# Attention into a gated FFN on one core: the first batch in another order of loads, bias copies, masks and P V

## The chip, the cores and the metric

The kernel runs on one core of a Trainium2 chip. The metric is the time of one execution on the device, in microseconds (us). Three runs of the kernel before gave 438.77, 437.65 and 438.74, so a median of 438.74 us.

## What is computed

There are 8 batches of 8 heads, 576 positions and 64 numbers per head. Each head is a causal attention with a bias that falls with the distance between two positions, and its result, 4608 tokens by 512, goes through a gated FFN of width 1536:

```python
scores = q @ k.T / 8
cum = np.cumsum(np.maximum(s, 0), axis=-1)
scores += np.minimum(-(cum[:, None] - cum[None, :]), 0)   # and -1e9 above the diagonal
attn = softmax(scores) @ v
x = attn of all heads side by side                          # 4608 x 512
g = x @ w_gate
out = (g * sigmoid(g) * (x @ w_val)) @ w_out
```

## The kernel before

**The scores.** TensorE multiplies k (as weights) by q in one pass with a contraction of 128 rows: 64 rows hold k and q of a head, and 4 of the other 64 hold the bias. There the cumulative sum, times 8, stands as a coarse and a fine bf16 row (tile `HL`), against rows of 1 and -1, so that the product adds their difference. The tiles `KQ[i][e]` hold this: `i` is the buffer, `e` tells which half of the rows is q and k; one tile serves heads 0 and 2 of a group of four ("half batch", `hb`), the other heads 1 and 3. `aug` (L159) copies the bias rows of one half batch by DMA.

**One head** is four score pieces (L250), an exponential of each on ScalarE (L258), two masks of the diagonal blocks on GpSimd (L262, L267), then 15 small multiplications of the probabilities `pt` by V (L283, "P V"), whose last column of ones gives the row sums, and on VectorE a reciprocal and a multiplication (L298, L299). The PSUM tile of P V has one buffer, so that a head's P V waits until VectorE has read the one before. Every two heads, `x_pe` (L315) transposes the result into the FFN's input.

**Preparing k, q and V.** SyncE's queue (SP) loads them in fp32. GpSimd casts k and q to bf16 (`cast_one`, L174), TensorE transposes them (`pe_transpose`, L206), and VectorE and ScalarE copy them from PSUM to `KQ` (L217, L215). V is cast to the tile `VT` (L221). The buffer of raw V is single, those of raw k and q are double.

**The order** is written out by hand: each engine and each DMA queue takes its instructions in the order of the code. First come loads, memsets, the bias and half batch 0. Then `attn_items` gives the attention in pieces, and `pump` runs it up to a position. All eight heads of batch 0 run before the FFN's first tile of 512 tokens, since that tile needs all heads of its tokens; after that one piece of FFN (36 of them per tile) alternates with attention of the following batch. `side` holds what is issued beside a head: k and q of the next half batch, loads of V and the weights. The weights come in 12 DMAs from GpSimd's queue, which converts them from fp32 to bf16: four parts each of gate ("g"), value ("v") and output ("o").

Of the kernel before, what the change touches and what calls it, by code (L numbers as in the profile page):

```python
# [12 lines left out]
FP32 = mybir.dt.float32  # L13
# [6 lines left out]
def kernel(  # L20
# [79 lines left out]
    HL = const.tile([BH, 2, S], BF16)  # L100
    warm = const.tile([128, 1], FP32)

    with tc.manual_schedule():
# [30 lines left out]
        load_qk(0)  # L134
        load_v(0, range(5))
        load_qk(1)
# [184 lines left out]

        def side(h, step):
            if h == 0:
                if step == 0:
                    w_load("g", 1)
                    cast_one(1, "k", 0, nc.gpsimd)
                    cast_one(1, "q", 0, nc.gpsimd)
                if step == 1:
                    w_load("v", 1)
                    cast_one(1, "k", 1, nc.gpsimd)  # L330
                    cast_one(1, "q", 1, nc.gpsimd)
                if step in (2, 3):
                    for nm in ("k", "q"):
                        pe_transpose(1, nm, step - 2, (nc.vector, nc.vector))
                if step == 3:
                    w_load("g", 2)
                return
            if h == 1:
                if step == 0:
                    aug(2, nc.sync)  # L340
                    load_qk(2)
                    load_v(1, range(5))
                    w_load("v", 2)
                if step == 1:
                    w_load("g", 3)
                if step == 2:
                    w_load("v", 3)
                if step == 3:
                    w_load("o", 0)
# [36 lines left out]
        def attn_items():  # L386
            for kk in range(BH + 4):
                first = kk < H + 2
                bh = kk if first else kk - 2
                b_lo, b_hi = (0, H) if first else (H, BH)  # L390
                h, step = divmod(bh, HB)
                if not first and step == 0 and 2 <= h < NPE:
                    if h > 2:
                        aug(h, nc.sync)
# [19 lines left out]
                x = bh - 2  # L414
# [3 lines left out]
                p = bh - 1  # L418
# [137 lines left out]
```

## Time and profile before

| | |
|---|---|
| median of 3 runs | 438.74 us |
| the profiled execution | 440.81 us, of which the span from the first to the last instruction 439.1 us |
| TensorE busy | 394.4 us (90%) |
| VectorE, ScalarE, GpSimd busy | 265.7, 208.0, 138.8 us (61%, 47%, 32%) |
| chain that ended last | TensorE 84%, VectorE 10% |
| mean granted TensorE clock | 0.979 |

Engines are named PE (TensorE), DVE (VectorE), ACT (ScalarE), POOL (GpSimd) and SP (SyncE's queue). The page cuts the span into 40 slices of 11 us; a digit is the busy share of an engine in tenths. TensorE has `0538888696` in the first ten slices and 9 nearly everywhere after. VectorE has `7588` in the first four. The DMA engines stand at `8975999767` there. So the time in which TensorE isn't full lies in the first quarter, and the rows below come from there.

### The profile page before, as it was taken

To read this page: it belongs to the slowest core of one execution; us is meant where nothing else is said; L and a number is where in the kernel's file an instruction comes from. 1 tells how busy PE (TensorE), PEld (TensorE's weight loads), DVE (VectorE), ACT (ScalarE), POOL (GpSimd) and SP (SyncE) were. 2 spreads that over 40 slices of the span, in tenths; PEclk is the share of its full clock that TensorE was granted. 3 is DMA by queue.
4 is the path that set the end of the run, shared out by engine and by line. 5 is a ranking of instruction groups with operands and counts; after the bars stand their busy time and mean duration, and the time that the engine had idled before them with its cause. 6 is when DMAs were issued, how large, how long until landed. Compare 5 with 4: busy or idle time off the path is not lost.

```text
span 439.1 us, 8204 instructions
## 1 busy us (share of the span) xinstructions
PE 394.4 (90%) x3112; PEld 217.2 (49%) x3112; DVE 265.7 (61%) x507; ACT 208.0 (47%) x418; POOL 138.8 (32%) x249
## 2 busy tenths in 40 slices
PE   0538888696899999999999999999999999999996
PEld 0326545354455555555555555555555554444442
DVE  7588475634269637963794479448935762780760
ACT  1424447544455555555655555456555551332331
POOL 0753813446334423443262416241721110000000
PEclk9999899979699999999999999999999999999999
DMA  8975999767588659756965796577431001002002
GB/s 185 191 106 98 203 202 221 125 147 187 137 190 184 133 136 228 159 119 190 194 152 120 201 192 155 131 188 162 69 90 50 1 1 72 24 2 86 11 0 96
DMA packets 92679, 56.42 MB, mean 128 GB/s; under 512 B 65568, under 2 KB 87968, under 8 KB 92640
## 3 DMA queue, kind: packets, MB, share of 16 engines
q1 hardware_dynamic: 86672, 51.16, 51.5%
q0 software_dynamic: 5952, 4.73, 7.2%
q8 instruction: 24, 0.39, 0.4%
q14 instruction: 15, 0.12, 0.1%
q10 hardware_dynamic: 16, 0.01, 0.0%
HBM read 37.90 MB, written 15.93 MB: 123 GB/s over the span
## 4 chain that ended last, share of the span: by engine, by line
PE 84%; DVE 10%; ACT 2%; issue 2%; POOL 1%; DMA 0%; SPq 0%; ACTq 0%
PE py L459 22%; PE pv L448 21%; PE pg L435 21%; PE sc L250 9%; PE av L283 7%; DVE kq L217 4%; PE xps L315 3%; DVE vt L221 1%; DVE kq L148 1%; DVE kq L147 1%; ACT pt L258 1%; DVE ot L299 1%; DVE kq L146 1%; POOL kq L164 1%; DVE pp L442 0%
## 5 line engine op out<-in xcount | busy, mean ns | idle before, releaser
L258 ACT ACTIVATE pt<-sc 128x512 bf16<-128x512 f32 (+1 forms) x256 | 117.3, 504 | 68.2 <-PE sc L250 67.4
L448 PE MATMUL pv<-xt,wv 128*128 128x512 bf16 x432 | 113.3, 385 | 0.0
L435 PE MATMUL pg<-xt,wg 128*128 128x512 bf16 x432 | 112.6, 384 | 0.0
L442 DVE SCALAR_TENSOR_TENSOR pp<-th,pg 128x512 bf16<-128x512 bf16 x108 | 74.2, 687 | 61.1 <-ACT th L440 60.7
L440 ACT ACTIVATE th<-pg 128x512 bf16<-128x512 f32 x108 | 64.5, 597 | 90.7 <-PE pg L435 90.7
L459 PE MATMUL py<-wo,ht 128*128 128x512 bf16 x432 | 107.4, 384 | 0.0
L250 PE MATMUL sc<-kq 128*128 128x128 bf16 (+4 forms) x576 | 78.5, 253 | 11.7 <-DMA kq<-HL 4.7
L262 POOL TENSOR_SCALAR_AFFINE_SELECT pt<-pt 128x512 bf16<-128x512 bf16 x64 | 41.1, 642 | 141.3 <-ACT pt L258 141.2
L453 DVE TENSOR_TENSOR ht<-pp,pv 128x512 bf16<-128x512 bf16 x108 | 73.9, 684 | 13.0 <-PE pv L448 4.4
L250 PEld LDWEIGHTS <-kq 128*128 128x128 bf16 x576 | 48.0, 103 | 45.6 <-issue 6.5
L283 PE MATMUL av<-vt,pt 128*128 128x65 bf16 x960 | 51.8, 199 | 10.7 <-DVE ot L299 9.1
L448 PEld LDWEIGHTS <-wv 128*128 128x128 bf16 x432 | 39.3, 99 | 38.4 <-issue 4.1
L283 PEld LDWEIGHTS <-pt 128*128 128x128 bf16 x960 | 43.2, 101 | 29.2 <-issue 11.5
L435 PEld LDWEIGHTS <-wg 128*128 128x128 bf16 x432 | 38.8, 99 | 36.8 <-issue 1.8
L459 PEld LDWEIGHTS <-ht 128*128 128x128 bf16 x432 | 38.4, 99 | 35.8 <-issue 1.1
L467 ACT ACTIVATE ysb<-py 128x512 f32<-128x512 f32 x36 | 21.5, 597 | 44.8 <-PE py L459 42.7
L298 DVE RECIPROCAL rc<-av 128x5 f32<-128x5 f32 x64 | 12.2, 191 | 37.6 <-PE av L283 37.4
L267 POOL TENSOR_SCALAR_AFFINE_SELECT pt<-pt 128x64 bf16<-128x64 bf16 x64 | 15.3, 240 | 60.2 <-ACT pt L258 60.1
L299 DVE TENSOR_TENSOR ot<-av,rc 128x320 bf16<-128x320 f32 x64 | 31.5, 492 | 2.2
L319 DVE COPY xt<-xps 128x64 bf16<-128x64 bf16 (+7 forms) x32 | 9.8, 305 | 35.3 <-PE xps L315 35.3
L221 POOL CAST vt<-rawv 128x512 bf16<-128x512 f32 (+1 forms) x35 | 23.1, 677 | 10.9 <-DMA rawv<-in_v_dram 10.8
L174 POOL CAST ck<-rawk 96x768 bf16<-96x768 f32 x32 | 26.1, 833 | 0.0
(37 smaller groups left out, 174.9 us busy)
## 6 DMA issues: line engine op xcount, KB each, us to landing
rawk<-in_k_dram SPq DMA_DIRECT2D x16, 576.0 KB
rawq<-in_q_dram SPq DMA_DIRECT2D x16, 576.0 KB
out_dram<-ysb SPq DMA_DIRECT2D x36, 256.0 KB
rawv<-in_v_dram SPq DMA_DIRECT2D x32, 256.0 KB
ks<-ck SPq DMA_DIRECT2D x11, 288.0 KB
qs<-cq SPq DMA_DIRECT2D x11, 288.0 KB
kq<-HL SPq DMA_DIRECT2D x120, 2.2 KB
wg<-in_moe_w_gate_dram POOLq DMA_DIRECT2D x4, 384.0 KB, 5.3
```

The source lines that it names most:

```text
L221: eng.tensor_copy(VT[b % 2][0:n, c, :, 0:D], loaded["v", b][0:n, c, :, :])
L250: nc.tensor.matmul(sc[:, o : o + w], T[:, 0, r * S + 128 * tj : r * S + 128 * (tj + 1)], T[:, 1, r * S + lo : r * S + hi], start=True, sto ...
L258: nc.scalar.activation(pt[:, CHUNK_PT[ci] : CHUNK_PT[ci] + o], sc[:, 0:o], AF.Exp, scale=0.125)
L262: nc.gpsimd.affine_select(pt[:, 1088:1600], pt[:, 1088:1600], pattern=[[0, 4], [1, 128]], compare_op=ALU.is_ge, fill=zreg, base=0, channel ...
L283: nc.tensor.matmul(av[:, bi * (D + 1) : (bi + 1) * (D + 1)], pt[:, c0 : c0 + 128], VT[b % 2][:, tj, h, :], start=(tj == 0), stop=(tj == bi),)
L299: nc.vector.tensor_mul(ot[:, :, e * D : (e + 1) * D], av3[:, :, 0:D], rc[:, :, None].to_broadcast([128, NCH, D]),)
L435: nc.tensor.matmul(pg, WG[j][:, c, f0 : f0 + 128], xt[:, c, :], start=(c == 0), stop=(c == 3),)
L440: nc.scalar.activation(th, pg, AF.Tanh, scale=0.5)
L442: nc.vector.scalar_tensor_tensor(pp, in0=th, scalar=1.0, in1=pg, op0=ALU.add, op1=ALU.mult)
L448: nc.tensor.matmul(pv, WV[j][:, c, f0 : f0 + 128], xt[:, c, :], start=(c == 0), stop=(c == 3),)
L453: nc.vector.tensor_mul(ht, pp, pv)
L459: nc.tensor.matmul(py, hts[ft][:, ts_ * 128 : (ts_ + 1) * 128], WO[ft // 3][:, ft % 3, :], start=(ft == 0), stop=(ft == NFT - 1),)
```

## The change

It concerns the first batch and what is issued around it.

- `HL` gets four row pairs, so that one DMA per head carries the rows of the sum and those of 1 and -1, for k and q together (8 rows of 576 numbers); before it took two DMAs of 2 rows, and the 1 and -1 came from memsets.
- The memsets of `KQ` are cut down (fp32 writes of a pair of bf16 ones in one), partly moved to GpSimd, and partly placed later. VectorE's bias chain comes ahead of them.
- On SP k and q of half batch 1 load ahead of V.
- GpSimd casts k and q of half batch 0 ahead of the bias DMAs, and then issues weight parts g0, v0, the bias copies of half batch 1, and g1, v1, ahead of the first mask. The other eight weight parts follow one per head, behind the mask of heads 1 to 8.
- In batch 0 P V comes three heads behind the scores instead of one. V is cast on VectorE once head 3 has been issued.
- The bias copies and loads of half batches 2 and 3 are issued within batch 0.
- In the first FFN tile attention starts with the first pieces of the FFN (`n0 = 0`) and not with the eighth.


```diff
-    HL = const.tile([BH, 2, S], BF16)
+    HL = const.tile([BH, 4, 2, S], BF16)
...
         load_qk(0)
+        load_qk(1)
         load_v(0, range(5))
-        load_qk(1)
...
+        PAIR_ONE = 1.0019378662109375
+
+        def aug_rows(i, e):
+            r0 = 64 * (1 - e)
+            return KQ[i][e][r0 : r0 + 64, :, :].bitcast(FP32)
...
-        def init_kq(i, eng):
-            for e in range(2):
-                T = KQ[i][e]
-                r0 = 64 * (1 - e)
-                eng.memset(T[r0 : r0 + 64, 0, :], 0.0)
-                eng.memset(T[r0 : r0 + 2, 0, :], -1.0)
-                eng.memset(T[r0 : r0 + 64, 1, :], 1.0)
-                eng.memset(T[64 * e : 64 * e + 64, :, NR * S :], 0.0)
-
         nc.vector.memset(one_s, 1.0)
-        init_kq(0, nc.vector)
+        nc.vector.memset(HL[:, 2:4, 0, :].bitcast(FP32), -1.005844116210937500)
+        nc.vector.memset(HL[:, 0:2, 1, :].bitcast(FP32), PAIR_ONE)
+        for e in range(2):
+            nc.gpsimd.memset(aug_rows(0, e)[:, 1, :], PAIR_ONE)
+            nc.vector.memset(aug_rows(0, e)[:, 0, :], 0.0)
+        nc.gpsimd.memset(aug_rows(1, 0)[:, 1, :], PAIR_ONE)
...
-        nc.vector.tensor_copy(HL[:, 0, :], c8)
-        nc.vector.tensor_sub(HL[:, 1, :], c8, HL[:, 0, :])
-
-        def aug(hb, *engs):
+        nc.vector.tensor_copy(HL[:, 0, 0, :], c8)
+        nc.vector.tensor_sub(HL[:, 1, 0, :], c8, HL[:, 0, 0, :])
+        nc.vector.tensor_copy(HL[:, 2:4, 1, :], HL[:, 0:2, 0, :])
+
+        def aug(hb, engs):
             for hh in range(HB):
                 r, e = divmod(hh, 2)
-                for kq in range(2):
-                    a0 = 64 * (1 - e) + 2 - 2 * kq
-                    engs[kq % len(engs)].dma_start(
-                        KQ[hb % 2][e][a0 : a0 + 2, kq, r * S : (r + 1) * S],
-                        HL[hb * HB + hh : hb * HB + hh + 1, :, :],
-                    )
+                r0 = 64 * (1 - e)
+                engs[hh].dma_start(
+                    KQ[hb % 2][e][r0 : r0 + 4, :, r * S : (r + 1) * S],
+                    HL[hb * HB + hh : hb * HB + hh + 1, :, :, :],
+                )
...
+        wlate = {
+            1: ("g", 2), 2: ("v", 2), 3: ("g", 3), 4: ("v", 3),
+            5: ("o", 0), 6: ("o", 1), 7: ("o", 2), 8: ("o", 3),
+        }
+
         def side(h, step):
+            bh = HB * h + step
+            if bh in wlate:
+                w_load(*wlate[bh])
             if h == 0:
                 if step == 0:
-                    w_load("g", 1)
-                    cast_one(1, "k", 0, nc.gpsimd)
-                    cast_one(1, "q", 0, nc.gpsimd)
+                    for r in range(NR):
+                        cast_one(1, "k", r, nc.gpsimd)
+                        cast_one(1, "q", r, nc.gpsimd)
                 if step == 1:
-                    w_load("v", 1)
-                    cast_one(1, "k", 1, nc.gpsimd)
-                    cast_one(1, "q", 1, nc.gpsimd)
-                if step in (2, 3):
                     for nm in ("k", "q"):
-                        pe_transpose(1, nm, step - 2, (nc.vector, nc.vector))
+                        pe_transpose(1, nm, 0, (nc.vector, nc.vector))
+                if step == 2:
+                    for nm in ("k", "q"):
+                        pe_transpose(1, nm, 1, (nc.vector, nc.vector))
                 if step == 3:
-                    w_load("g", 2)
+                    for c in range(5):
+                        cast_v(0, c, nc.vector)
+                    load_qk(2)
                 return
             if h == 1:
                 if step == 0:
-                    aug(2, nc.sync)
-                    load_qk(2)
+                    aug(2, SP4)
                     load_v(1, range(5))
...
         def attn_items():
-            for kk in range(BH + 4):
-                first = kk < H + 2
-                bh = kk if first else kk - 2
+            for kk in range(BH + 6):
+                first = kk < H + 4
+                bh = kk if first else kk - 4
+                lag = 3 if first else 1
...
+                if first and bh == H:
+                    load_qk(3)
+                    aug(3, SP4)
...
-                x = bh - 2
+                x = bh - lag - 1
...
-                p = bh - 1
+                p = bh - lag
...
-        aug(0, nc.scalar, nc.gpsimd)
         for r in range(NR):
             cast_one(0, "k", r, nc.gpsimd)
+        for r in range(NR):
             cast_one(0, "q", r, nc.gpsimd)
-        for r in range(NR):
-            pe_transpose(0, "k", r, (nc.vector, nc.scalar))
-            pe_transpose(0, "q", r, (nc.vector, nc.scalar))
+        aug(0, [nc.scalar, nc.gpsimd, nc.scalar, nc.gpsimd])
+        nc.gpsimd.memset(aug_rows(1, 1)[:, 1, :], PAIR_ONE)
+        for e in range(2):
+            nc.vector.memset(aug_rows(1, e)[:, 0, :], 0.0)
+        pe_transpose(0, "k", 0, (nc.scalar, nc.scalar))
+        pe_transpose(0, "k", 1, (nc.scalar, nc.scalar))
+        pe_transpose(0, "q", 0, (nc.vector, nc.vector))
+        pe_transpose(0, "q", 1, (nc.vector, nc.vector))
         w_load("g", 0)
         w_load("v", 0)
-
-        def init_vt(i):
+        aug(1, [nc.gpsimd] * 4)
+        w_load("g", 1)
+        w_load("v", 1)
...
-        init_vt(0)
-        for c in range(5):
-            cast_v(0, c, nc.vector)
-        init_kq(1, nc.vector)
-        aug(1, nc.sync)
-        init_vt(1)
...
-        start = H + 1.45
+        start = H + 3.45
...
-            n0 = 7 if tt == 0 else 0
+            n0 = 0
```

VectorE at the program's start. Before, the memsets of the four tiles stand ahead of the bias (L146 to L149; here those of the second tile, `kq10`, which repeat the first's), which begins with `s_sb`:

```order
L146 MEMSET kq10_128 64x608
L147 MEMSET kq10_128 2x1216
L148 MEMSET kq10_128 64x1216
L149 MEMSET kq10_128 64x2x32
L154 TENSOR_SCALAR s_sb_134<-s_sb_134 64x576
L155 SCALAR_TENSOR_TENSOR c8_136<-one_s_135,s_sb_134 64x576
L156 CAST HL_137<-c8_136 64x576
L157 TENSOR_TENSOR HL_137<-c8_136,HL_137 64x576
L217 COPY kq00_127<-tps_189 64x576
L217 COPY kq00_127<-tps_198 64x576
```

Now, on the same engine from the third instruction on:

```order
L148 MEMSET HL_137 64x2x288
L149 MEMSET HL_137 64x2x288
L152 MEMSET kq00_127 64x608
L152 MEMSET kq10_128 64x608
L155 TENSOR_SCALAR s_sb_134<-s_sb_134 64x576
L156 SCALAR_TENSOR_TENSOR c8_136<-one_s_135,s_sb_134 64x576
L157 CAST HL_137<-c8_136 64x576
L158 TENSOR_TENSOR HL_137<-c8_136,HL_137 64x576
L159 COPY HL_137<-HL_137 64x2x576
L488 MEMSET kq01_129 64x608
L488 MEMSET kq11_130 64x608
L220 COPY kq00_127<-tps_206 64x576
```

The memsets of 1216 numbers are gone, two of `HL` and a copy have come in, and the copies of half batch 0 that follow are those of q alone.

GpSimd behind the casts of half batch 0, before (`wg0`, `wv0`: weight parts; L262, L267: the masks of a head; `ck_265`, `cq_267`: casts of half batch 1):

```order
L232 DMA wg0_115<-in_moe_w_gate_dram 128x4x384
L232 DMA wv0_119<-in_moe_w_val_dram 128x4x384
L262 AFFINE_SELECT pt_252<-pt_252 128x512
L232 DMA wg1_116<-in_moe_w_gate_dram 128x4x384
L174 CAST ck_265<-rawk_152 96x2x6x64
L174 CAST cq_267<-rawq_154 96x2x6x64
L267 AFFINE_SELECT pt_252<-pt_252 128x64
L262 AFFINE_SELECT pt_277<-pt_277 128x512
L232 DMA wv1_120<-in_moe_w_val_dram 128x4x384
L174 CAST ck_265<-rawk_152 96x2x6x64
```

Now (L165: bias copies of half batch 1; L265: the first mask; `ck_252`, `cq_254`: casts of half batch 1):

```order
L486 MEMSET kq11_130 64x608
L235 DMA wg0_115<-in_moe_w_gate_dram 128x4x384
L235 DMA wv0_119<-in_moe_w_val_dram 128x4x384
L165 DMA kq01_129<-HL_137 4x2x576
L165 DMA kq11_130<-HL_137 4x2x576
L165 DMA kq01_129<-HL_137 4x2x576
L165 DMA kq11_130<-HL_137 4x2x576
L235 DMA wg1_116<-in_moe_w_gate_dram 128x4x384
L235 DMA wv1_120<-in_moe_w_val_dram 128x4x384
L265 AFFINE_SELECT pt_240<-pt_240 128x512
L177 CAST ck_252<-rawk_146 96x2x6x64
L177 CAST cq_254<-rawq_148 96x2x6x64
```

Four bias copies and the weight parts g1 and v1 now stand ahead of the first mask and of half batch 1's casts.

The SP queue from its start, before (`s`, then k and q of half batch 0, V, k and q of half batch 1, bias copies):

```order
L133 DMA s_sb_134<-in_s_dram 64x576
L110 DMA rawk_142<-in_k_dram 96x4x384
L110 DMA rawq_144<-in_q_dram 96x4x384
L128 DMA rawv_146<-in_v_dram 128x8x64 x4
L128 DMA rawv_146<-in_v_dram 64x8x64
L110 DMA rawk_152<-in_k_dram 96x4x384
L110 DMA rawq_154<-in_q_dram 96x4x384
L164 DMA kq01_129<-HL_137 2x1x576 x2
L164 DMA kq11_130<-HL_137 2x1x576 x2
```

Now:

```order
L133 DMA s_sb_134<-in_s_dram 64x576
L110 DMA rawk_142<-in_k_dram 96x4x384
L110 DMA rawq_144<-in_q_dram 96x4x384
L110 DMA rawk_146<-in_k_dram 96x4x384
L110 DMA rawq_148<-in_q_dram 96x4x384
L128 DMA rawv_150<-in_v_dram 128x8x64 x4
L128 DMA rawv_150<-in_v_dram 64x8x64
L110 DMA rawk_362<-in_k_dram 96x4x384
L110 DMA rawq_364<-in_q_dram 96x4x384
L165 DMA kq00_127<-HL_137 4x2x576
L165 DMA kq10_128<-HL_137 4x2x576
```

V has moved behind k and q of half batch 1, and the loads of half batch 2 stand ahead of the bias copies.

## Rows read from the trace of the kernel before

**Rows 1.** Busy time by stretch: us, length, busy (instructions), granted clock, DMA

```profile
0.00:44.00 44.00, 18.26 (x171) 13.67 (x171) 33.08 (x53) 13.79 (x29) 18.61 (x35) 1.00 0.80 145
...
52.00:55.00 3.00, 3.00 (x8) 1.02 (x8) 1.21 (x3) 0.60 (x1) 3.00 (x5) 0.54 1.27 191
...
60.00:68.00 8.00, 5.34 (x51) 3.27 (x49) 5.63 (x9) 5.34 (x11) 0.97 (x2) 1.00 1.20 204
...
80.00:90.00 10.00, 6.01 (x59) 3.80 (x58) 5.25 (x10) 4.83 (x9) 3.28 (x6) 0.82 0.64 126
...
122.00:150.00 28.00, 28.00 (x231) 15.41 (x230) 23.32 (x44) 16.13 (x33) 12.52 (x22) 1.00 0.84 177
```

**Rows 2.** TensorE in order of time: start, us, line, count, idle before

```profile
15.15 0.66 PE L206 MATMUL tps<-ident,ck 96*128 96x96 bf16 x6 [15.15 <-POOL ck L174]
...
18.12 1.44 PE L250 MATMUL sc<-kq 128*128 128x128 bf16 x8
...
33.53 0.98 PE L283 MATMUL av<-vt,pt 128*128 128x65 bf16 x15 [6.22 <-DVE ot L299]
...
51.90 1.61 PE L435 MATMUL pg<-xt,wg 128*128 128x512 bf16 x4
```

**Rows 3.** VectorE in order of time, first 25 us

```profile
1.02 0.54 DVE L151 MEMSET one_s<- 64x576 f32 x1
...
2.60 1.07 DVE L147 MEMSET kq<- 2x1216 bf16 x1 [0.31 <-DVE kq L146]
...
8.60 0.45 DVE L154 TENSOR_SCALAR s_sb<-s_sb 64x576 f32<-64x576 f32 x1
...
10.95 0.75 DVE L157 TENSOR_TENSOR HL<-c,HL 64x576 bf16<-64x576 f32 x1
...
15.85 3.05 DVE L217 COPY kq<-tps 64x576 bf16<-64x576 bf16 x4 [4.15 <-PE tps L206]
...
19.75 5.01 DVE L221 CAST vt<-rawv 128x512 bf16<-128x512 f32 x5
...
21.21 2.59 DVE L221 CAST vt<-rawv 128x512 bf16<-128x512 f32 x1
```

**Rows 4.** GpSimd in order of time

```profile
12.00 2.26 POOL L164 DMA_DIRECT2D kq<-HL  x4 [10.63 <-DVE HL L157]
...
14.26 0.84 POOL L174 CAST ck<-rawk 96x768 bf16<-96x768 f32 x1
...
17.34 0.79 POOL L232 DMA_DIRECT2D wg<-in_moe_w_gate_dram  x1
...
21.72 0.84 POOL L174 CAST ck<-rawk 96x768 bf16<-96x768 f32 x1
...
63.56 0.62 POOL L221 CAST vt<-rawv 128x512 bf16<-128x512 f32 x1 [5.88 <-DMA rawv<-in_v_dram]
```

**Rows 5.** DMA queue q1, 3 to 12 us: packets, MB, share

```profile
q1 hardware_dynamic: 4403, 2.06, 111.6%
```

**Rows 6.** DMA queues, 52 to 60 us

```profile
q0 software_dynamic: 1366, 1.20, 91.1%
...
q1 hardware_dynamic: 1364, 0.34, 32.5%
```

**Rows 7.** DMA issues to 95 us, GpSimd's bias copies: us to landing

```profile
kq<-HL POOLq DMA_DIRECT2D x4, 2.2 KB, 6.1
```

**Rows 8.** TensorE in order of time, after the FFN's start

```profile
61.37 0.42 PE L206 MATMUL tps<-ident,ck 96*128 96x96 bf16 x6
...
87.29 1.89 PE L448 MATMUL pv<-xt,wv 128*128 128x512 bf16 x4
...
93.88 1.03 PE L459 MATMUL py<-wo,ht 128*128 128x512 bf16 x4
...
111.58 1.44 PE L250 MATMUL sc<-kq 128*128 128x128 bf16 x8 [4.73 <-DMA kq<-HL]
```

**Rows 9.** The SP queue at 109 us

```profile
108.94 4.96 SPq L164 DMA_DIRECT2D kq<-HL  x8
```

More of the change, by code (lines that the diff above doesn't have):

```diff
@@ L140 @@
         make_identity(nc, ident)
-        def init_kq(i, eng):
-            for e in range(2):
-                T = KQ[i][e]
-                r0 = 64 * (1 - e)
-                eng.memset(T[r0 : r0 + 64, 0, :], 0.0)
-                eng.memset(T[r0 : r0 + 2, 0, :], -1.0)
-                eng.memset(T[r0 : r0 + 64, 1, :], 1.0)
-                eng.memset(T[64 * e : 64 * e + 64, :, NR * S :], 0.0)
-        nc.vector.memset(one_s, 1.0)
-        init_kq(0, nc.vector)
+        nc.vector.memset(one_s, 1.0)
+        nc.vector.memset(HL[:, 2:4, 0, :].bitcast(FP32), -1.005844116210937500)
[4 more added lines that the diff above has]
+        nc.gpsimd.memset(aug_rows(1, 0)[:, 1, :], PAIR_ONE)
         nc.vector.tensor_scalar(s_sb, s_sb, 0.0, 8.0, ALU.max, ALU.mult)
         nc.vector.tensor_tensor_scan(c8, one_s, s_sb, 0.0, ALU.mult, ALU.add)
-        nc.vector.tensor_copy(HL[:, 0, :], c8)
-        nc.vector.tensor_sub(HL[:, 1, :], c8, HL[:, 0, :])
-        def aug(hb, *engs):
+        nc.vector.tensor_copy(HL[:, 0, 0, :], c8)
+        nc.vector.tensor_sub(HL[:, 1, 0, :], c8, HL[:, 0, 0, :])
+        nc.vector.tensor_copy(HL[:, 2:4, 1, :], HL[:, 0:2, 0, :])
+        def aug(hb, engs):
             for hh in range(HB):
                 r, e = divmod(hh, 2)
-                for kq in range(2):
-                    a0 = 64 * (1 - e) + 2 - 2 * kq
-                    engs[kq % len(engs)].dma_start(
-                        KQ[hb % 2][e][a0 : a0 + 2, kq, r * S : (r + 1) * S],
-                        HL[hb * HB + hh : hb * HB + hh + 1, :, :],
-                    )
+                r0 = 64 * (1 - e)
[3 more added lines that the diff above has]
+                )
+        SP4 = [nc.sync] * 4
         cts = {}
@@ L339, in side @@
                 if step == 0:
-                    aug(2, nc.sync)
-                    load_qk(2)
+                    aug(2, SP4)
                     load_v(1, range(5))
[L343 to L349, printed above, removed]
                 return
@@ L355, in side @@
                     split(h + 1, "k", nc.vector)
-                    aug(h + 1, nc.sync)
+                    aug(h + 1, SP4)
                 if step == 1:
@@ L392, in attn_items @@
                 if not first and step == 0 and 2 <= h < NPE:
-                    if h > 2:
-                        aug(h, nc.sync)
+                    if h > 3:
+                        aug(h, SP4)
                     for nm in ("k", "q"):
@@ L471, in ffn_items @@
                 yield 1
-        aug(0, nc.scalar, nc.gpsimd)
         for r in range(NR):
             cast_one(0, "k", r, nc.gpsimd)
+        for r in range(NR):
             cast_one(0, "q", r, nc.gpsimd)
-        for r in range(NR):
-            pe_transpose(0, "k", r, (nc.vector, nc.scalar))
-            pe_transpose(0, "q", r, (nc.vector, nc.scalar))
+        aug(0, [nc.scalar, nc.gpsimd, nc.scalar, nc.gpsimd])
[6 more added lines that the diff above has]
+        pe_transpose(0, "q", 1, (nc.vector, nc.vector))
         w_load("g", 0)
         w_load("v", 0)
-        def init_vt(i):
+        aug(1, [nc.gpsimd] * 4)
+        w_load("g", 1)
+        w_load("v", 1)
+        for i in range(2):
             nc.vector.memset(VT[i][:, :, :, D : D + 1], 1.0)
             nc.vector.memset(VT[i][64:128, 4, :, 0:D], 0.0)
-        init_vt(0)
-        for c in range(5):
-            cast_v(0, c, nc.vector)
-        init_kq(1, nc.vector)
-        aug(1, nc.sync)
-        init_vt(1)
+        for e in range(2):
+            for i in range(2):
+                nc.vector.memset(KQ[i][e][64 * e : 64 * e + 64, :, NR * S :], 0.0)
         at = attn_items()
@@ L504 @@
         LAG = 1.65
-        start = H + 1.45
+        start = H + 3.45
         pump(start)
         hook = {
-            1: [lambda: w_load("o", 1)],
-            3: [lambda: w_load("o", 2)],
-            5: [lambda: w_load("o", 3)],
-            9: [lambda: load_qk(3)],
             21: [lambda: load_qk(4)],
@@ L514 @@
         for tt in range(NTT):
-            lo = start if tt == 0 else H * (tt + 1) + 2 + LAG
-            hi = min(H * (tt + 2) + 2 + LAG, BH + 4)
+            lo = start if tt == 0 else H * (tt + 1) + 4 + LAG
+            hi = min(H * (tt + 2) + 4 + LAG, BH + 6)
             span = 36
-            n0 = 7 if tt == 0 else 0
+            n0 = 0
             n = 0
```

## The prediction

> **What bounds the kernel now.** I read the table of busy time by stretch first, to see where TensorE isn't full. From 122 us on it is full to the end of the attention [rows 1], so only the 122 us before can change much. In the first 44 us it is busy for 18.3, and then come two holes: 2.7 of 8 us from 60 to 68 and 4.0 of 10 us from 80 to 90 [rows 1]. TensorE's timeline names the waits: 15.15 us for the first cast, 6.22 us at 33.5 for VectorE, and 4.73 us at 111.6 for a bias DMA [rows 2, 8]. The FFN starts at 51.90 [rows 2]. What runs after that is the same set of instructions in both kernels, so the time changes by the shift of this start and by the holes behind it.
>
> Who makes batch 0 late? VectorE, 33.1 of 44 us busy [rows 1]. Its timeline has eight memsets of 1.07 us like the one at 2.60; the bias chain starts at 8.60 and ends at 11.7; then come casts of V (5.0 us) and the second half of the memsets, behind which head 0's reciprocal waits [rows 3]. GpSimd sits idle 10.6 us for the bias rows and casts only behind its four bias copies, at 14.26 [rows 4].
>
> **The change, part by part. Up to the scores.** VectorE's prelude is now five memsets of some 0.55 us (0.54 for the one at 1.02 [rows 3]) from 1.02, with gaps near 0.2: 4.6 us. The old chain from 8.60 to 11.70 takes 3.1 more, and the copy within `HL` (1152 numbers; the subtraction of 576 took 0.75, so 0 to 1.5 us, I take 0.9): bias rows at 8.6 instead of 11.7.
>
> s, k and q of half batch 0 are 1.33 MB. SP's queue moved 2.06 MB from 3 to 12 us, 0.229 MB/us [rows 5]; an estimate from that, with little moved before 3 us, has them landed at 8. Casts, 0.84 each [rows 4], end at 9.7, where they ended near 17.4. The bias copies took 6.1 us to land beside full queues [rows 7], so the first scores start at about 14.7 (8.6 + 6.1) where they started at 18.12 [rows 2]. But the next link is GpSimd: from 9.7 two bias copies (0.57 each: 2.26 for four [rows 4]), a memset (not shown on this engine; between 0 and a cast's 0.84, I take 0.7), g0 and v0 (0.79 each), four bias copies, g1, v1: 17.0. Then the first mask, below 0.84, and the four casts of half batch 1: 21. In the kernel before the first of these casts started at 21.72 [rows 4]. Eight copies on VectorE at 0.76 (3.05 for four) follow from about 19.5: 25.5; the V casts at 5.0 then end at 30.5 [rows 3]. That is the floor of this path.
>
> **V's landing** is what I think sets the end instead. SP has to move s and all of k and q first, 2.51 MB: 13.2 us at 0.229. GpSimd's weight queue is filled from 11.5 on and, with the time that a weight took to land, runs from about 14. What do the two do to one another? From 52 to 60 us, where the second V load and the weights ran together, they took turns packet by packet (1366 to 1364), so that the weights moved 1.20 MB and V, in its short pieces, 0.34: 0.150 and 0.043 MB/us [rows 6]. The cast of a V block there waited 5.88 us for its landing [rows 4]. A weight part is 0.39 MB, 2.6 us at 0.150. Seven (g0, v0, g1, v1, and g2, v2, g3 behind the masks of heads 1 to 3) keep the queue full from 14.2 to 32.5; the eighth hangs on head 4's mask, behind the first P V. V (1.18 MB) has 0.23 before 14.2 and 18.3 x 0.043 = 0.79 beside the weights; the last 0.16 takes 0.7 alone. V lands at 33.2, its last cast ends at 34.2, and head 0's P V at 34.4. Bounds: V unhindered, and then the floor of 30.5; V at 0.043 throughout after 14.2, 36.3, and P V at 37.4.
>
> **From the first P V to the FFN.** Before, 18.4 us passed from 33.53 to 51.90 [rows 2], with seven P V, five heads of scores, a set of transposes for half batch 1 and four transposes of results. Now the same without one head of scores and that set. A head's scores took about 1.4 us at that stage's pace and the set about 1, which makes 16; with fewer gaps in the score part I take 15.5. The FFN starts at 34.4 + 15.5 = 49.9: **2.0 us earlier**, between 5.4 earlier (30.5 + 0.2 + 15.8 = 46.5) and 1.5 later (37.4 + 16 = 53.4).
>
> **Behind the FFN's start.** (1) Half batch 2 is now transposed after three pieces of FFN instead of nine; before, 9.5 us of pure FFN lay between [rows 2, 8]. In the first 3 us the granted clock was 0.54, mostly the 1.2 GHz level, after P V had paused for VectorE; the 2.7 us hole that follows at 60 to 68 left the clock at 1.00 [rows 1]. Now that hole comes some 4 us after the start, when the clock has hardly come back. Price: 0 if the clock comes back anyway, 3 if it falls as it did at 87 us (below). I take 2.0 **later**. (2) Half batch 3: before, an FFN group stood between the transposes of k and of q, with VectorE's FFN step between its copies, and the hole was 4.0 us. Now all four sets stand behind one FFN group, as at half batch 2 before, whose hole was 2.7: **1.3 earlier**. After the 4.0 us hole four FFN multiplications took 1.89 us instead of 1.03 [rows 8], and some 6 us ran at half speed, which costs about **2.9**; the hole of 2.7 brought no fall, so I count it as saved (0 at worst). (3) Half batch 4: TensorE waits 4.73 us for a bias copy [rows 8], behind SP's transposing loads. The copies are as late as before relative to the work, but one FFN group more (0.9 us) lies ahead, and head 16 needs one copy instead of two at 0.62 (4.96 for eight [rows 9]): **1.5 earlier**, between 0 and 4.7. (4) Eight bias copies fewer per pair of half batches on SP, later on: no TensorE wait hangs on them after 122 us [rows 1], so nothing.
>
> Sum: -2.0 + 2.0 - 1.3 - 2.9 - 1.5 = -5.7. From the profiled span 439.1 that is 433.4, so 435.1 for that execution (440.81); it ran 2.1 above the median, from which I take the same 5.7: 433.0 us.
>
> **A rule that speaks against it.** One of VectorE's five V casts took 2.59 us, the other four together 2.4, and in that stretch GpSimd cast k and q [rows 3, 4]. The Trainium skill ("SBUF — State Buffer", section "Who interferes with whom") says that a copy or cast on VectorE in its two-port mode and a GpSimd instruction shut one another out for a whole instruction. The trace agrees with it there. In the new order GpSimd's masks and weight DMAs run beside the V casts; by that rule the last cast, on which P V waits, could take up to 2.0 us more, and the result would be 435.0. I count nothing for it: most casts wait for V's landing anyway.
>
> **Rivals.** *V isn't the limit.* If the weight queue runs dry between g1/v1 and g2, V catches up five times as fast as beside them (0.229 against 0.043), and the floor of 30.5 decides. For it: g2 comes behind head 1's mask, at about 22, only 2 us before the first four parts end. Start 46.5, result 433.0 - 3.4 = 429.6. 18%.
>
> *V is starved to its bound, and the clock saves nothing.* All the gain ahead of the P V is waited away: FFN start at 53.4 (+1.5), the holes behind it gain only what the order says, -1.3 and -1.5, and the clock stays as it is: 437.4. For it: the wait for V is the same kind as the 5.88 us. Against it: the masks hold the eighth weight back. 20%, half of it above 437.4.
>
> *The second batch's V is starved (slower).* Place: raw V has one buffer, so batch 1's V is issued once batch 0's has been cast (34.2), and behind half batch 2's k and q, which land by about 41. GpSimd's masks stand behind all five casts of it. Four weight parts (v3, o0, o1, o2) run beside it, 10.5 us in which V gets 0.45 MB; the rest takes 3.4 alone: about 55. Head 8's mask is needed near 60. If it moved at 0.043 throughout, it would land at 68 and hold TensorE some 7.5 us: 433.0 + 7.5 = 440.5. It decides from a landing after 60, and from 65 on it undoes the whole gain. Against it: the weights run out first. 8%.
>
> **Chances and range.** The forecast has 54%, the two rivals that stay faster or equal 18 and 20, the slower one 8. About 0.3%, or 1.3 us, is what can be told from no change: faster means below 437.4, slower above 440.1. Faster: 54 + 18 + 10, less 1 for the forecast's own tail: 81%. Within: 11%. Slower: 8%. The forecast's own terms reach from 429.6 to 437.4 by the bounds of V's landing and the clock; with part of either side the range is 427.5 to 438.5.
>
> **What would show it.** First scores near 15 us and the casts of half batch 1 near 18 to 21 confirm GpSimd's queue. V casts on VectorE that wait for the DMA, with blocks some 6 us apart and the last near 33, confirm the landing; casts back to back ending near 30 make the first rival right. The FFN should start near 50, TensorE's first half at the lower level, and the holes should stand at about 54 (2.7 us or more), 80 (2.7) and 105 (3). I am wrong if P V starts before 28, if TensorE waits on a mask of head 8, or if a hole stands somewhere else, as at the transposes of half batch 4, whose raw q now loads behind half batch 5's cast.

## The result and the profile after

The changed kernel takes 426.92 us (median of 4 runs, 425.59 to 427.82) beside 438.75 for the kernel before on the same chip: ratio 0.9732, 95% interval 0.9701 to 0.9763. That is 11.8 us, where 5.7 were forecast. The profiled execution took 426.86, its span 425.2 against 439.1.

TensorE's timeline of the changed kernel, answering [rows 2, 8] (start, us, line, count, idle before):

```profile
16.27 1.49 PE L253 MATMUL sc<-kq 128*128 128x128 bf16 x9 [4.66 <-DVE kq L503]
...
20.30 0.66 PE L209 MATMUL tps<-ident,ck 96*128 96x96 bf16 x6 [1.19 <-POOL ck L177]
...
27.74 1.58 PE L286 MATMUL av<-vt,pt 128*128 128x65 bf16 x15 [1.19 <-DVE vt L224]
...
44.41 0.77 PE L318 MATMUL xps<-ident,ot 128*128 128x128 bf16 x5 [0.81 <-DVE ot L302]
45.52 1.49 PE L443 MATMUL pg<-xt,wg 128*128 128x512 bf16 x3 [0.33 <-issue]
...
50.39 0.41 PE L209 MATMUL tps<-ident,cq 96*128 96x96 bf16 x6 [0.64 <-DVE pp L450]
51.72 0.82 PE L253 MATMUL sc<-kq 128*128 128x128 bf16 x8 [0.91 <-DVE kq L220]
...
54.33 0.19 PE L253 MATMUL sc<-kq 128*128 128x64 bf16 x1 [0.93 <-ACT pt L261]
...
71.51 0.41 PE L209 MATMUL tps<-ident,cq 96*128 96x96 bf16 x6 [0.64 <-DVE pp L450]
72.84 0.83 PE L253 MATMUL sc<-kq 128*128 128x128 bf16 x8 [0.92 <-DVE kq L220]
...
75.45 0.19 PE L253 MATMUL sc<-kq 128*128 128x64 bf16 x1 [0.91 <-ACT pt L261]
...
96.71 1.46 PE L253 MATMUL sc<-kq 128*128 128x128 bf16 x8 [2.86 <-DMA kq<-HL]
...
106.42 0.81 PE L443 MATMUL pg<-xt,wg 128*128 128x512 bf16 x3
```

The last transposes of batch 0 end at 45.2, and the FFN follows; it started at 51.90 [rows 2]: 6.7 us earlier. (The line at 45.52 lists three of that group's four multiplications; one has no record.) The first `pg` of the second FFN tile starts at 106.42, against 120.28 before. That is 13.9 earlier, the whole difference of the spans; so next to nothing changed behind it, and 7.2 us came between the FFN's start and there. The busy table for exactly this stretch (us, length, then PE, PEld, DVE, ACT, POOL busy, granted clock), first before, then after:

```profile
51.90:120.28 68.38, 56.31 (x458) 31.42 (x457) 33.87 (x66) 34.09 (x68) 27.83 (x47) 0.88 0.84 171
```

```profile
45.18:106.42 61.24, 51.21 (x449) 29.88 (x458) 33.26 (x66) 34.59 (x68) 25.22 (x44) 0.93 0.79 176
```

Full speed less the granted clock, times the length, is 8.2 us lost before and 4.3 now: 3.9 of the 7.2. The waits named in the timeline went from 12.0 us (2.7, 3.9 and 5.4 at half batches 2, 3 and 4) to 9.3 (2.8, 2.5 and 4.1): 2.7. By stage, answering [rows 1]:

```profile
45.18:47.00 1.82, 1.49 (x5) 0.67 (x6) 0.52 (x2) 0.00 (x0) 0.00 (x0) 0.50 1.23 198
47.00:52.00 5.00, 3.45 (x38) 2.21 (x36) 3.72 (x6) 2.13 (x4) 1.23 (x2) 0.96 1.10 212
52.00:60.00 8.00, 6.72 (x53) 3.60 (x52) 3.88 (x7) 6.21 (x13) 3.70 (x7) 1.00 1.08 219
...
70.00:80.00 10.00, 7.48 (x77) 4.62 (x77) 6.52 (x12) 7.29 (x14) 3.63 (x6) 1.00 0.51 120
80.00:90.00 10.00, 9.90 (x98) 5.90 (x98) 4.75 (x12) 5.22 (x12) 6.86 (x14) 1.00 0.60 159
```

The hole of half batch 3 is now 2.5 us in 70 to 80, and the clock behind it stays at 1.00, where it was 0.82 in the stretch with the hole [rows 1] and 0.84 in the next one of the kernel before:

```profile
90.00:100.00 10.00, 10.00 (x84) 5.54 (x82) 3.64 (x10) 4.63 (x11) 5.82 (x10) 0.84 0.45 108
```

What released the first P V? VectorE and GpSimd of the changed kernel, in order of time, answering [rows 3, 4]:

```profile
21.00 6.14 DVE L220 COPY kq<-tps 64x576 bf16<-64x576 bf16 x8 [4.68 <-PE tps L209]
27.17 1.89 DVE L224 CAST vt<-rawv 128x512 bf16<-128x512 f32 x5
```

```profile
12.18 0.62 POOL L486 MEMSET kq<- 64x608 f32 x1
...
17.26 0.78 POOL L235 DMA_DIRECT2D wg<-in_moe_w_gate_dram  x1 [0.67 <-DMA kq<-HL]
...
18.80 0.68 POOL L265 TENSOR_SCALAR_AFFINE_SELECT pt<-pt 128x512 bf16<-128x512 bf16 x1
19.39 0.85 POOL L177 CAST ck<-rawk 96x768 bf16<-96x768 f32 x1
```

The V casts follow the copies with no wait for V. Their queue, answering [rows 5, 6] (packets, MB), from 14 to 16, 16 to 20 and 20 to 23 us:

```profile
q1 hardware_dynamic: 1381, 0.35, 121.9%
q0 software_dynamic: 84, 0.03, 12.9%
```

```profile
q0 software_dynamic: 766, 0.58, 92.3%
q1 hardware_dynamic: 754, 0.19, 35.7%
```

```profile
q0 software_dynamic: 568, 0.36, 75.1%
q1 hardware_dynamic: 1060, 0.27, 53.1%
```

Beside the weights (q0) V moves 0.048 MB/us, packet for packet, as in [rows 6]. But the weights begin only between 15 and 16 us, and up to 16 the queue carried 3.16 MB (0.19 to 3 us, 2.18 from 3 to 12, 0.79 from 12 to 16); less the 2.51 of s, k and q, 0.65 of it is V. From 20 to 23 the weights leave it some room. With 0.65 + 0.19 + 0.27 of 1.18 MB by 23 us, and 0.07 more in the next, V has landed at about 24.

### The profile page after: what moved, and what is told of

It is laid out like the page before. It is cut to its first block, busy times and chain, and to the rows that moved or that the text cites. A ratio compares the mean times of both kernels' runs of the same rounds, so it can differ in the third digit from the quotient of the medians.

```text
span 425.2 us, 8041 instructions
## 1 busy us (share of the span) xinstructions
PE 387.1 (91%) x3058; PEld 215.3 (51%) x3112; DVE 255.1 (60%) x502; ACT 208.3 (49%) x418; POOL 142.1 (33%) x255
## 4 chain that ended last, share of the span: by engine, by line
PE 87%; DVE 4%; DMA 4%; issue 2%; ACT 1%; POOL 1%; SPq 0%; ACTq 0%
PE py L467 22%; PE pg L443 22%; PE pv L456 21%; PE sc L253 10%; PE av L286 8%; DVE kq L220 3%; PE xps L318 3%; DMA kq<-HL 2%; DMA rawq<-in_q_dram 2%; ACT pt L261 1%; DVE ot L302 1%; POOL cq L177 0%; DVE pp L450 0%; ACT th L448 0%; DVE rc L301 0%
## 5 line engine op out<-in xcount | busy, mean ns | idle before, releaser
L443 PE MATMUL pg<-xt,wg 128*128 128x512 bf16 x414 | 109.8, 381 | 1.3 <-issue 0.3
L456 PE MATMUL pv<-xt,wv 128*128 128x512 bf16 x412 | 109.6, 380 | 1.0
L467 PE MATMUL py<-wo,ht 128*128 128x512 bf16 x416 | 104.9, 383 | 1.0 <-issue 0.2
L265 POOL TENSOR_SCALAR_AFFINE_SELECT pt<-pt 128x512 bf16<-128x512 bf16 x64 | 40.6, 635 | 130.1 <-ACT pt L261 129.8
```

What stands on the lines that cost most here:

```text
L265: nc.gpsimd.affine_select(pt[:, 1088:1600], pt[:, 1088:1600], pattern=[[0, 4], [1, 128]], compare_op=ALU.is_ge, fill=zreg, base=0, channel ...
L443: nc.tensor.matmul(pg, WG[j][:, c, f0 : f0 + 128], xt[:, c, :], start=(c == 0), stop=(c == 3),)
L456: nc.tensor.matmul(pv, WV[j][:, c, f0 : f0 + 128], xt[:, c, :], start=(c == 0), stop=(c == 3),)
L467: nc.tensor.matmul(py, hts[ft][:, ts_ * 128 : (ts_ + 1) * 128], WO[ft // 3][:, ft % 3, :], start=(ft == 0), stop=(ft == NFT - 1),)
```

## The experiments

Times of the kernel before beside them are 439.7 to 439.9 us. Each edit is to the changed kernel unless it says otherwise.

**The changed kernel again.**

> The changed kernel itself, unedited, as the measure for the runs beside it on this chip. Both theories: 0.973 of the kernel before, so 427 to 428 us where that takes 439 to 440.

427.39 us (426.78 to 427.85), ratio 0.9725 (0.9705 to 0.9745). In this profile the clock did fall at half batch 2, unlike in the one above, and already behind the first two waits of its hole (0.64 and 0.91 us, as above): the scores that follow took 1.22 us instead of 0.82.

```profile
47.00:52.00 5.00, 3.45 (x35) 2.08 (x34) 3.23 (x6) 1.53 (x3) 0.69 (x2) 0.84 1.18 219
52.00:60.00 8.00, 7.76 (x52) 4.13 (x51) 3.71 (x6) 6.28 (x13) 3.50 (x7) 0.79 1.08 210
```

From 44 to 60 us that is 4.0 us lost to the clock against 1.8 in the other execution. The FFN had started 1.2 earlier (44.35 against 45.52), so the times lie close together.

**Half batch 2 later again: eight pieces of FFN first.**

```
-            n0 = 0
+            n0 = 7 if tt == 0 else 0
```

> The changed kernel with the first FFN tile's attention held back by seven pieces again (n0 = 7), nothing else undone. Theory A (order of the FFN pieces makes the holes behind the FFN's start): the FFN still starts at 45.2 us; an FFN group stands between the transposes of k and q of half batch 3 again, the hole there grows from 2.5 to about 4 us and the clock falls after it (2.9 us), so 426.9 + 1.4 + 2.9 = 431 us, 430 to 432.5. Rival B (the holes shrank because bias copies and loads of half batches 2 and 3 are issued earlier): holes as in the changed kernel, 427 us, within 1.

432.25 us (431.31 to 432.78), ratio 0.9835 (0.9811 to 0.986): 4.9 us slower than the changed kernel. The FFN starts as early (44.28), but the holes and the clock of before are back: at half batch 3

```profile
75.46 0.41 PE L209 MATMUL tps<-ident,cq 96*128 96x96 bf16 x6 [0.53 <-ACT kq L218]
77.46 0.82 PE L253 MATMUL sc<-kq 128*128 128x128 bf16 x8 [1.59 <-DVE kq L220]
80.08 0.21 PE L253 MATMUL sc<-kq 128*128 128x64 bf16 x1 [1.80 <-ACT pt L261]
...
102.63 1.46 PE L253 MATMUL sc<-kq 128*128 128x128 bf16 x8 [4.55 <-DMA kq<-HL]
```

with a granted clock of 0.86 from 80 to 90. So 4.9 of the 7.2 us gained behind the FFN's start hang on this one number.

**That number alone, in the kernel before.**

```
-            n0 = 7 if tt == 0 else 0
+            n0 = 0
```

> The kernel before with one line of the change alone: attention from the FFN's first piece on (n0 = 0). The FFN starts at 51.9 as before. Theory A: half batch 3's hole shrinks from 4.0 to 2.6 us and brings no fall of the clock (-4.3 in all), but batch 1's V lands as late as before, 67.6 us, and head 8's P V now stands at about 66 instead of 70.6, so that TensorE waits there some 4 us behind GpSimd's casts of V, perhaps with a fall of the clock: net -1 to +2, 437.5 to 441. Rival B (the change of order pays by itself): no wait at head 8, 434 to 435.

436.81 us (434.49 to 437.35), ratio 0.9931 (0.9907 to 0.9955): 3.0 us, and neither theory is right. The hole of half batch 3 shrinks little, since the scores there wait for something else:

```profile
82.76 1.44 PE L250 MATMUL sc<-kq 128*128 128x128 bf16 x8 [2.87 <-ACT kq L215]
```

```profile
65.50 14.21 SPq L128 DMA_DIRECT2D rawv<-in_v_dram  x5
79.81 5.08 SPq L164 DMA_DIRECT2D kq<-HL  x8
```

The bias copies of half batch 3 are issued from 79.81 to 84.9, behind SP's V loads, and the scores begin at 82.76, between them. That fits a wait for the first of these copies, though the timeline names ScalarE, whose four copies end at 82.75: in the changed kernel the same scores start at 72.84, when ScalarE has done one of four. In the DMA view V's 256 B pieces run until 82, and the first four packets of 512 B or more, the rows of two bias copies, come between 81.2 and 82.0. It was not tried alone.

**Are the early bias copies of half batch 3 needed in the changed kernel?** They go back behind the start of their half batch (`h > 2`, and `aug(3, SP4)` at `bh == H` removed).

> The changed kernel with half batch 3's bias copies issued where the kernel before has them, at its first head, behind the load of the third V on SP. Theory A (the early copies and the order of the FFN pieces are both needed at half batch 3): the FFN starts at 44 to 45.2, the hole at half batch 3 grows from 2.5 to 3.5 to 4.5 us and the clock falls behind it, 429 to 432. Rival B (the order of the pieces alone closed the hole): no change, 427.

427.13 us (one run): no difference, and the hole is the same 2.5 us (0.64, 0.91, 0.92). In the changed kernel the copies are early enough at their old place: SP is through with the third V at 66.54, 3.1 us ahead of half batch 3's transposes (69.65), while in the run above it was through at 79.71, 1.8 us behind them (77.91). What of the order moves that V was not tried.

**Is V's landing the limit? V later, behind half batch 2's k and q.**

```
-        load_v(0, range(5))
...
-                    load_qk(2)
...
+        load_qk(2)
+        load_v(0, range(5))
         w_load("g", 0)
```

> The changed kernel with V of batch 0 one place later on SP, behind k and q of half batch 2, so that it starts at about 17 us, beside the weights from the first byte. Theory A (the price of 0.043 to 0.05 MB/us for V beside the weights was right, and V escaped it in the changed kernel because it began before them): the weight queue stays full to about 34, V lands at 35 to 37, VectorE's casts wait for it, the first P V of head 0 ends at 37 to 38 instead of 29.3, the FFN starts at 52 to 54 and the kernel takes 434 to 436. Rival B (V's landing never matters, the weights don't hold it): V lands at 17 + 1.18/0.229 = 22 to 23, nothing moves, 427.

436.48 us (one run), FFN start 55.89. Here V is the limit, and it looks as the prediction drew it:

```profile
31.41 0.43 DVE L223 CAST vt<-rawv 128x512 bf16<-128x512 f32 x1 [1.64 <-DMA rawv<-in_v_dram]
36.87 0.43 DVE L223 CAST vt<-rawv 128x512 bf16<-128x512 f32 x1 [5.03 <-DMA rawv<-in_v_dram]
39.31 0.42 DVE L223 CAST vt<-rawv 64x512 bf16<-64x512 f32 x1 [2.01 <-DMA rawv<-in_v_dram]
```

**V earlier, ahead of half batch 1's k and q.**

```
-        load_qk(1)
         load_v(0, range(5))
+        load_qk(1)
```

> The changed kernel with V loaded ahead of k and q of half batch 1 again (SP's order of before). Theory A (the path goes through GpSimd's queue, whose casts of half batch 1 come at 19.4 to 22.5, and not through SP's order): k of half batch 1 lands by 17 and q by about 20 to 21 beside the weights, so the casts wait 0 to 1 us, the FFN starts at 45 to 46.5, and the kernel takes 426.5 to 428.5. Rival B (loading q and k of both halves ahead of V is what gave the gain): the transposes of half batch 1 come 4 us or more later, the FFN starts after 49, 431 or more.

429.87 us (one run), some 2.5 above the repeat of the changed kernel, between the theories. V's casts run without a wait for the DMA, but take 2.68 us instead of 1.89, and GpSimd's queue comes later: there a weight load waits 1.61 us for a bias copy, instead of 0.67.

```profile
19.31 0.77 POOL L235 DMA_DIRECT2D wv<-in_moe_w_val_dram  x1 [1.61 <-DMA kq<-HL]
```

Half batch 1's casts, none of which waits for its load, start at 20.67 instead of 19.39, and its first transposes at 21.56 instead of 20.30.

**GpSimd freed of half batch 0's bias copies: all four on ScalarE.**

```
-        aug(0, [nc.scalar, nc.gpsimd, nc.scalar, nc.gpsimd])
+        aug(0, [nc.scalar] * 4)
```

> The changed kernel with all four bias copies of half batch 0 issued by ScalarE, so that GpSimd's queue ahead of the first mask loses two (1.34 us) and its wait of 0.67 us for one to land. Theory A (GpSimd's queue up to half batch 1's casts sets the first P V, not V's landing): the casts come 1 to 2 us earlier than 19.4, the FFN starts at 43.5 to 44.5 instead of 45.2, about 1 us less in all. Rival B (V's landing sets it): the weights start 1.3 us earlier, V lands later by some 2 us, the V casts wait, the FFN starts at 45.2 or later.

429.18 us (one run), 1.8 above the repeat of the changed kernel, with the FFN's first line at 47.12 instead of 45.52. The copies start 1.8 us earlier (19.17), but the weights, too, are issued earlier, and V is caught:

```profile
19.17 6.14 DVE L220 COPY kq<-tps 64x576 bf16<-64x576 bf16 x8 [2.79 <-PE tps L209]
...
27.65 0.43 DVE L224 CAST vt<-rawv 128x512 bf16<-128x512 f32 x1 [1.08 <-DMA rawv<-in_v_dram]
30.30 0.42 DVE L224 CAST vt<-rawv 64x512 bf16<-64x512 f32 x1 [2.22 <-DMA rawv<-in_v_dram]
```

So the prediction's limit stands just behind the one that held.

**Only g1 and v1 behind half batch 1's casts** (the two `w_load` lines moved into the step with the casts).

> The changed kernel with weight parts g1 and v1 behind half batch 1's casts on GpSimd, so that the casts come 1.6 us earlier, as in the run with the bias copies on ScalarE, but the weights later instead of earlier. Theory C (both limits stand close together: GpSimd's queue decides, with V's landing 1 to 2 us behind, and the weights' start moves V's landing by more than their own shift): V lands earlier than in the changed kernel, the V casts run without waits and end 1.5 us earlier, and the FFN starts 1 to 2 us earlier: 425 to 426.5. Rival B (V's landing alone decides): the FFN starts earlier by what the weights are later, 3 us or more. Rival D (the first scores decide, since the mask and so the casts wait for them): no change.

426.46 us (425.71 to 426.58), ratio 0.9703 (0.9677 to 0.9728): 0.9 below the repeat, within the intervals. The copies start 1.5 earlier and nothing waits for V, but the five casts take 2.65 instead of 1.89. VectorE's casts of this kernel, and GpSimd's work beside them:

```profile
L224 DVE CAST vt<-rawv 128x512 bf16<-128x512 f32 x4 | 2.3, 641 | 0.0
```

```profile
25.85 0.85 POOL L265 TENSOR_SCALAR_AFFINE_SELECT pt<-pt 128x512 bf16<-128x512 bf16 x1
```

A cast took 641 ns in the mean, against 450 in the changed kernel, where GpSimd idled beside most of them, and the mask 0.85 us against 0.63.

**Half batch 1's casts ahead of the weights, bias copies behind g0 and v0.** Its transposes move as well, ahead of the first scores.

> The changed kernel with half batch 1's casts on GpSimd directly behind the first bias copies, ahead of the weights, and its transposes ahead of the first scores. Theory A: the casts run at about 12.5 to 16 as k and q land (11.5 and 13.8), VectorE's eight copies end at 22 to 23 instead of 27.1, V has landed by then since the weights start 3 us later, the first P V ends at 25 instead of 29.3, and the FFN starts at 40.5 to 42: 3 to 4.5 us less than the changed kernel, 423 to 424 where that takes 427. Rival B (V's landing sets it): the first P V moves by what the weights are later alone, below 1 us.

426.84 us (425.52 to 428.07), ratio 0.9713 (0.9686 to 0.9741). P V starts 4.5 us earlier, and gives it back at once, at the scores of half batch 1:

```profile
23.19 1.53 PE L286 MATMUL av<-vt,pt 128*128 128x65 bf16 x15 [0.23 <-DVE vt L224]
...
28.76 1.56 PE L253 MATMUL sc<-kq 128*128 128x128 bf16 x9 [4.04 <-DMA kq<-HL]
```

**Bias copies, too, ahead of the weights.** The transposes stay where the run above has them; shown is GpSimd's queue.

```
+        aug(1, [nc.gpsimd] * 4)
+        for nm in ("k", "q"):
+            for r in range(NR):
+                cast_one(1, nm, r, nc.gpsimd)
         w_load("g", 0)
         w_load("v", 0)
-        aug(1, [nc.gpsimd] * 4)
```

> As the run with half batch 1 early (casts ahead of the weights, transposes ahead of the scores), but with half batch 1's bias copies ahead of those casts too, so that they don't land behind the weights. Theory A: the 4 us wait at head 4's scores goes, the first P V ends at 25 to 26 and the FFN starts at 40.5 to 42: 423 to 424.5 where the changed kernel takes 427.4. Rival B (GpSimd's queue of weights in flight holds the masks back instead): the FFN starts after 43.5, 426 or more.

425.89 us (424.2 to 427.13), ratio 0.9686 (0.9651 to 0.9721). The FFN starts at 41.36, but head 8's P V then waits 1.68 and 0.46 us for a mask on GpSimd, which stands behind casts of the second batch's V that wait 4.35, 5.28 and 5.72 us for their blocks.

**A second PSUM buffer for P V in batch 0.** TensorE waits 0.8 to 0.9 us for each `ot` of the tail, as at 44.41 above; odd heads now use a buffer of another pool.

```
+                if bh < H and bh % 2:
+                    avs[bh] = mp.tile([128, NCH * (D + 1)], FP32, tag="m", name="avm")
```

> The changed kernel with P V of batch 0's odd heads in a PSUM buffer of the pool that the FFN uses later, so that a head's P V needn't wait until VectorE has read the one before. Theory A (the stretch from the first P V to the FFN is bound by that one buffer, 3.5 us of waits at its end): the FFN starts 3 to 4 us earlier, at 41.5 to 42, and the clock falls less ahead of it: 422.5 to 424 where the changed kernel takes 427. Rival B (the scores and exponentials of heads 4 to 7 bound that stretch): below 1 us.

423.46 us (422.69 to 424.75), ratio 0.9645 (0.9616 to 0.9674). The FFN starts at 42.29, and the granted clock is 1.00 from 38 to 68 us, where the changed kernel has 0.50 from 44 to 47. The pauses ahead of it are half as many (one of 0.98 for two heads).

**Both together.**

> The run before with the second PSUM buffer for P V of batch 0 as well. Theory A: both gains add: the FFN starts at 37.5 to 39.5, and 419.5 to 421.5 follow. Rival B (the second V, which starts only when the first has been cast, then lands too late for head 8): TensorE waits 2 to 5 us at head 8's P V, 422 to 424.

426.71 us (425.67 to 428.08), ratio 0.9709 (0.9677 to 0.9741): the FFN starts at 38.45, 6.7 before the changed kernel, and the end is the same. The second V is starved, and the clock falls behind the wait:

```profile
56.48 0.84 PE L289 MATMUL av<-vt,pt 128*128 128x65 bf16 x12 [3.46 <-POOL pt L265]
```

```profile
52.00:60.00 8.00, 4.37 (x31) 2.30 (x29) 2.17 (x5) 1.56 (x4) 3.57 (x7) 0.72 1.11 231
60.00:68.00 8.00, 7.95 (x56) 4.16 (x55) 4.72 (x8) 4.92 (x11) 1.60 (x4) 0.85 1.02 200
```

**The same with four weight parts later, and the control.** The control has the second PSUM buffer and the later weights, but half batch 1 as in the changed kernel.

```
-            5: ("o", 0), 6: ("o", 1), 7: ("o", 2), 8: ("o", 3),
+            8: ("o", 0), 9: ("o", 1), 10: ("o", 2), 11: ("o", 3),
```

> As the kernel with half batch 1's bias copies and casts first and with two P V buffers (426.71 us, FFN start at 38.45), but the four parts of the out-projection's weights are issued behind the masks of heads 8 to 11 instead of 5 to 8. Theory A (the second V's starvation is all that ate that kernel's lead): the weight queue runs dry near 37 us, the second V lands near 42 to 45 at the full rate of 0.229 MB/us, GpSimd's V casts end before 46, head 8's P V doesn't wait for its mask (3.46 + 0.17 us less), and TensorE's clock doesn't fall from 56 to 62 us (some 6 us at half speed, 3 us less): 426.7 - 3.6 - 3 = 420, between 419 and 421.5. Theory B (something else stands there as well: the masks' order on GpSimd, or the clock falls behind the 2.5 us hole of half batch 2 anyway): the V casts end early and the time stays above 423. Theory C (a late weight part becomes the new wait): TensorE waits for wo near 84 us and the time is above 425.

> The changed kernel with two P V buffers (423.46 us), and the same later weights, as the control. There head 8's P V didn't wait for a mask though the second V landed near 53. Theory A: the second V lands some 8 us earlier (V casts end before 46) and nothing waits for it, so the time stays: 423.5, between 422.3 and 424.7. Theory B (later weights help by themselves, through less contention for the bias copies of half batches 2 to 4 or a steadier clock): 420 to 422. Theory C (late weights cost): above 425.

The first: 419.68 us (419.32 to 420.04), ratio 0.9546 (0.953 to 0.9563), the shortest time measured here. Head 8's P V doesn't wait, and the clock stays:

```profile
50.98 1.03 PE L451 MATMUL pv<-xt,wv 128*128 128x512 bf16 x4
51.84 0.80 PE L289 MATMUL av<-vt,pt 128*128 128x65 bf16 x15
```

```profile
52.00:60.00 8.00, 7.95 (x75) 4.54 (x73) 6.18 (x12) 5.42 (x12) 4.85 (x10) 1.00 1.13 230
```

The time is that of theory A; one of its steps is not, since the V casts end at 50.8, not before 46 (the weights that remain kept V at 0.29 MB from 38 to 44 us). The mask was done at 51.3, half a microsecond before P V started, so this margin is thin. The control: 422.84 us (422.45 to 424.13), ratio 0.9626 (0.9606 to 0.9646), V casts 6.2 us earlier (the last at 46.69 against 52.92) and no measurable gain. So it is the wait of head 8 (3.6 us) and the clock behind it (3.4 us from 52 to 68) that ate 7 us of the front part's gain.

## Why the prediction was off

The direction was right. The step that failed is **V's landing**, the claim that V's last block, at 33.2, sets the first P V. The mechanism is real: V moves at 0.048 MB/us beside the weights (0.043 was used), and it did become the limit in two kernels (436.48 and 429.18 us). Its timing was mis-sized by two earlier terms and one later one. The weights began between 15 and 16 us, not at 14.2, and k and q were through before: V had some 0.65 MB ahead of them, not 0.23. The 0.53 MB that were left at 16 us would have taken 11 us at 0.048 MB/us, to 27; the room that the weights left from 20 to 23 us brought it to about 24, as read above. V landed some 5 us ahead of the end of its last cast instead of 4 behind the floor; the 18% rival (V isn't the limit) is what happened, by V's head start more than by the gap between the weights that it named.

That rival's own floor, last cast at 30.5, was 1.4 too late: the copies began at 21.0 instead of 19.5 (+1.5: half batch 0's casts ended at 10.9, not 9.7, and GpSimd's queue waited 0.67 us for a bias copy in flight), and the V casts took 1.89 instead of 5.0 (-3.1). The 5.0 was read from a stretch where GpSimd cast k and q beside them [rows 3, 4]. The first scores, at 16.27 for 14.7, held nothing up: the first mask, at 18.80, followed GpSimd's weight loads without a wait.

From the end of head 0's P V (29.3) to the FFN (45.2) 15.9 us passed; 15.5 to 16 were given. The **first P V to FFN** step was right. Of the 4.7 us by which the FFN's start was off (-6.7 for -2.0), V's landing made 3.7 (34.2 against a floor of 30.5) and the floor 1.4, less 0.4 in this step.

**Half batch 2 (+2.0)** was the second wrong size: the hole is 2.8 us (0.64 + 0.91 + 0.93 + 0.30), 0.1 more than before, and the clock cost 1.1 us in the 16 us from the FFN's start on, where it had cost 1.7 before: -0.5 in all for +2.0. In the repeat it cost 4.0, 2.3 more than before, much as forecast. These are two executions of one kernel, so which of the two a run shows is luck as far as is known here.

**Half batch 3** was right: the hole went from 4.0 to 2.5 us (-1.5 for -1.3), and of the clock, 0.82 and 0.84 from 80 to 100 us before (3.4 us lost), nothing was lost behind it now (-3.4 for -2.9). The run with eight pieces first shows that both hang on the order; with half batch 4's wait, which comes back too (4.55), it costs 4.9 us. But the reason given, one FFN group between two sets of transposes, was only half of it: in the kernel before, without that group, the hole was still 3.5 us, and what fits there, though not tried alone, is that the late bias copies held it open.

**Half batch 4** was right: -1.3 (waits of 4.1 us instead of 5.4) for -1.5, with the clock behind it as before.

The terms as measured make -6.7 - 0.5 - 1.5 - 3.4 - 1.3 = -13.4, and the span shrank by 13.9; 0.5 us stays unassigned. The profiled execution of before ran 2.1 above its median, that of after at its median; so the medians differ by less than the spans.

The **slower rival** (the second V starved, head 8's mask late) didn't decide here: the last V cast ended at 54.3, and head 8's P V at 58.96 found its mask ready. The margin was some 4 us, and the kernels with an earlier FFN show it: 1.68 and 0.46 us of wait with a start at 41.36, 3.46 at 38.45, and none at 39.08 with the weights moved. The rule on two-port casts, counted at nothing, cost next to nothing in this kernel (one cast took 0.52 us, the others 0.41 to 0.42), because GpSimd waited 2.74 us for ScalarE during most of the casts. Where masks ran beside, the five casts took 0.8 us more, not 2.0: the longest took 0.86 us, and the mask 0.85 instead of 0.63. This agrees with the Trainium skill ("SBUF — State Buffer", section "Who interferes with whom") in that each of the two engines can hold up the other; that one is shut out for the other's whole instruction can't be read from it.

## What to carry to other kernels

Where two queues shared the DMA engines here, the one with the short pieces was starved (0.048 against 0.145 MB/us from 16 to 20 us), so work out when the other queue starts before saying who is late: with half batch 0's bias copies on ScalarE they were issued 1.3 us earlier (11.46 for 12.72), and V landed some 6 us later (30 for 24). Look at what stands 2 to 4 us behind the limit, since here each edit to half batch 1's order that removed one wait met the next one (bias copies, V, second V; 425.89 to 426.84 us). The second P V buffer alone gained 3.9 us, all of it together with the later weights 7.7. Read the price of an operation from a stretch with the same neighbours: the V casts cost 5.0, 2.65 or 1.89 us by what GpSimd did beside them.

## What the runs showed of the hardware

- GpSimd's bias copies took a median of 7.6 us from issue to landing in the changed kernel's first 95 us (5.9 the two that stand ahead of the weights on their queue, 8.0 the four behind two weight parts), and a weight load on GpSimd waited 0.67 us for one of them to land. In the kernel with half batch 1's casts first, two weight loads waited 1.49 and 2.88 us for an earlier weight part.
- Behind the same two waits (0.64 and 0.91 us) the granted clock was 1.00 from 52 to 60 us in one execution and 0.79 in another, of the same kernel. With half the pauses ahead of the FFN it was 1.00 from 38 to 44 us in two kernels (423.46 and 419.68 us) and 0.78 and 0.72 in two others (422.84 and 426.71), so the clock at the FFN's start, too, isn't fixed by the pauses alone.
- A memset of 64x608 fp32 numbers took 0.62 us on GpSimd and 0.56 on VectorE.
